# Weighing four value parts of eight on VectorE instead of three, in a two-layer decode kernel

## The chip, the cores and the metric

The kernel runs on one core of one Trainium2 chip. The metric is the time of one execution in device microseconds. The kernel before takes 2680.91 us (median of 3 runs, 2680.71 to 2681.0).

## What is computed

Two layers run one behind the other, each an attention block over a cache and a gated MLP, for two sequences with one new token each; both layers use the same weights and the same cache.

```python
def _A_ref(x, k_cache, v_cache, wq, wo):          # B=2, H=32, Sk=8192, Dh=128, D=576
    q = (x @ wq).reshape(B, Sq, H, Dh).transpose(0, 2, 1, 3)
    scores = einsum("bhqd,bhkd->bhqk", q, k_cache) * (Dh ** -0.5)
    p = softmax(scores, axis=-1)
    o = einsum("bhqk,bhkd->bhqd", p, v_cache)
    return o.transpose(0, 2, 1, 3).reshape(B, Sq, H * Dh) @ wo

def _B_ref(x, w_gate, w_up, w_down):              # Df=4608
    return (gelu(x @ w_gate) * (x @ w_up)) @ w_down

x = x + _A_ref(layernorm(x), ...);  x = x + _B_ref(layernorm(x), ...)
x = x + _A_ref(layernorm(x), ...);  x = x + _B_ref(layernorm(x), ...)
```

All is float32. The two caches hold 2 x 32 x 8192 x 128 numbers each, 268 MB apiece, and each layer reads both from HBM.

## The kernel before

**Items.** The attention of a layer is cut into 34 items: 30 of two heads of one sequence (item numbers 0 to 29) and 4 of one head. The first layer takes them in rising order, the second in falling order, and a few singles at the turn stay on the chip. For an item of two heads, each of the 128 partitions holds 128 rows of the keys (half of the partitions for each head), 128 x 128 numbers, in 8 parts of 16 rows. Keys and values of an item come with one transfer each, on SyncE's queue (`load`, L168), into one large tile, `space`. It has three places for such a block, each a pair of slots, and a transfer is issued when its whole pair is free. The keys of item i+1 go where the values of item i-2 were, the values of item i where its own keys were. The program is written out in order for each engine, and no scheduler changes that order.

**Keys.** `multiply` (L738) takes an item's keys in three units of 3, 3 and 2 parts. VectorE multiplies a unit with the query, which stands spread over all partitions in PSUM (L769), GpSimd adds the upper half of each row to the lower (L798), and VectorE sums what is left of each row (`add_up`, L801). The sum of one unit is taken after the product of the next one. The last unit's sum comes at the head of the next item's work, together with the maximum (`peak`, L825). The exponentials (`softmax`, ScalarE, L858) give the weights `prz`.

**Values, five parts of eight.** TensorE multiplies the weights with the values (`values`, L943): one product for each 4 of a partition's 128 rows, so 4 for a part, and 20 for five parts. In the profile each product of this kind is two rows.

**Values, the other three parts.** For the items that `folds` names (L893: items 3 to 26 in the first layer, 2 to 26 in the second, 49 together) VectorE weighs the rows of the last three parts with their weights (`weigh`, L911), which ScalarE has copied into the PSUM tile `share` (L905, in `bank2`), and GpSimd folds them: it halves the number of rows again and again (L914) until 4 are left, and adds the two results (L916). TensorE then adds up these 4 rows over the partitions with one product (`folded`, L921), which also sets the parts' place free. `weigh` is called twice for an item: with `first` behind the next item's third key product, and without it one item later, behind the last sum of the keys.

**Around it.** Item i's block in the loop (L1051) first sums the last unit of the keys of item i-1 and weighs for item i-2 (second call). Then it takes the three key units of item i, with the query of the next item and the folded product of item i-2 behind the first unit, the values of item i-1 and in every second item the gathering of a finished pair (L966, L967) behind the second, and the first call of `weigh` for item i-1 behind the third.

Of the kernel before, what the change touches and what calls it, by code (L numbers as in the profile page):

```python
# [24 lines left out]
JC = 16  # L25
# [18 lines left out]
END = RING + NPLACE * PLACE  # L44
HELD = 5
SPLIT = (18, 18, 12, 16)
FOLD = 3


class Item:  # L50
# [75 lines left out]
def decode_layers(ctx, tc, x_in, kc, vc, wq, wo, wg, wu, wd, out):  # L126
# [32 lines left out]
    def part_at(at, n):  # L159
        return space[:, at:at + n]  # L160
# [177 lines left out]
    def groups(layer):  # L338
        return range(H // WIDE[layer])[::1 - 2 * layer]

    def name(kind, layer, n):

        return kind, 1 if n in (KEYS_HELD if kind == "k" else VALUES_HELD) else layer, n
# [119 lines left out]
    for b in range(B):  # L463
        rows = ident.rearrange("p (c v i r) -> p i r v c", c=4, v=4, i=2)[:, :, :, b, :]
# [51 lines left out]
    low = bank2[:, 4 * GH + P + 6:]  # L516
    share = low[:, :FOLD * JC]
    kept = psum1.tile([P, JC, DH], F32, name="kept")
# [93 lines left out]
    def attention(layer):  # L612
# [224 lines left out]
        def weights_of(n):  # L837

            if ITEMS[n].heads == 2:
                return prz.rearrange("p a e -> p (a e)")  # L840
            return prz[:, n - PAIRS, :]
# [55 lines left out]
        def weigh(n, first):  # L897

            lo = ITEMS[n].parts - FOLD
            if first:  # L900
                of_halves = weights_of(n)[:, 8 + 4 * JC * lo:8 + 4 * JC * (lo + FOLD)]
                of_halves = of_halves.rearrange("p (g a e) -> p a g e", a=4, e=4)
                for i in range(2):
                    at = slice(i * HALF, i * HALF + HALF)
                    nc.scalar.copy(share[at].rearrange("p (g e) -> p g e", e=4), of_halves[at, i])  # L905
            begin, rows = (0, JC) if first else (JC, (FOLD - 1) * JC)
            at = arena.live[name("v", layer, n), lo][0]
            t = part_at(at, FOLD * PART).rearrange("p (j d) -> p j d", d=DH)
            of_rows = share[:, begin:begin + rows].unsqueeze(2).to_broadcast([P, rows, DH])
            u = t[:, begin:begin + rows]  # L910
            nc.vector.tensor_tensor(out=u, in0=u, in1=of_rows, op=ALU.mult)  # L911
            while rows > 4:
                rows //= 2
                nc.gpsimd.tensor_tensor(out=u[:, :rows], in0=u[:, :rows], in1=u[:, rows:2 * rows], op=ALU.add)  # L914
            if not first:
                nc.gpsimd.tensor_tensor(out=t[:, :4], in0=t[:, :4], in1=u[:, :4], op=ALU.add)  # L916

        def folded(n):

            key, lo = name("v", layer, n), ITEMS[n].parts - FOLD  # L920
            nc.tensor.matmul(  # L921
# [129 lines left out]
        for i, n in enumerate(seq):  # L1051
# [8 lines left out]
            first = layer == 1 and i == 1  # L1060
# [8 lines left out]
            if f is not None:  # L1069
                weigh(f, False)  # L1070
# [3 lines left out]
            for j, (k, m) in enumerate(us):  # L1074
# [28 lines left out]
                if j == 2 and i and folds(p):  # L1103
                    weigh(p, True)
# [14 lines left out]
        first, second = groups(layer)[:2]  # L1119
# [183 lines left out]
```

## Time and profile before

| | |
|---|---|
| median of 3 runs | 2680.91 us |
| the profiled execution | 2680.4 us, its span 2678.6 us |
| TensorE products, weight loads | busy 32%, 10% of the span |
| VectorE | 78% |
| GpSimd | 67% |
| ScalarE | 7% |
| DMA | 1153.33 MB at 431 GB/s on average, busy in tenths 9 or more in 39 of 40 slices |

In the tables by stage, each row gives the stretch in us from the start of the span, its length, the busy time of PE, PEld, DVE (VectorE), ACT (ScalarE) and POOL (GpSimd) with the number of instructions, TensorE's granted clock, the share of the DMA engines that was busy and GB/s. In a timeline, each row has the start, the duration, the engine, the line, the operation, output and inputs, the shape, and in brackets how long the engine was idle before and what ended that. SPq is SyncE's queue of transfers.

### The profile page before, as it was taken

How to read it: one execution, taken by the hardware profiler on the slowest of the kernel's cores; microseconds unless marked ns; L12 is line 12 of the kernel's file. 1: busy time of each engine (PE TensorE's matmuls, PEld its weight loads, DVE VectorE, ACT ScalarE, POOL GpSimd, SP SyncE). 2: the span in 40 equal slices, each digit the busy share in tenths (PEclk: the TensorE clock that was granted, in tenths of full speed). 3: DMA queues.
4: the chain of work that ended last, by engine and by line, in shares of the span. 5: the costliest groups of instructions: out<-in, count | busy, mean ns of one | idle time of the engine just before them, and what ended most of it. 6: DMA issues, size and time to landing. Idle time of an engine off the chain costs nothing.

```text
span 2678.6 us, 14389 instructions
## 1 busy us (share of the span) xinstructions
PE 848.9 (32%) x5550; PEld 269.3 (10%) x5550; DVE 2086.9 (78%) x916; ACT 185.0 (7%) x890; POOL 1797.4 (67%) x559
## 2 busy tenths in 40 slices
PE   1313232232223232334663322223222322222256
PEld 0100000000000000011221100000000000000022
DVE  4878888898888888867038779888888988888840
ACT  0000000000000000001026000000000000000000
POOL 2547787778778777844028458778887877787720
PEclk8666655665665566566986665566566556655678
DMA  9999999999999999999999999999999999999998
GB/s 423 437 429 434 435 433 433 433 436 433 431 435 434 430 436 431 434 429 426 419 417 432 435 437 429 434 434 433 433 433 436 430 433 437 428 436 436 430 431 383
DMA packets 29340, 1153.33 MB, mean 431 GB/s; under 512 B 3384, under 2 KB 3416, under 8 KB 4184
## 3 DMA queue, kind: packets, MB, share of 16 engines
q1 hardware_dynamic: 29088, 1152.40, 99.8%
q8 instruction: 43, 0.70, 0.1%
q14 instruction: 25, 0.20, 0.0%
q10 hardware_dynamic: 184, 0.02, 0.0%
HBM read 1152.39 MB, written 0.01 MB: 430 GB/s over the span
## 4 chain that ended last, share of the span: by engine, by line
DMA 70%; DVE 20%; PE 6%; POOL 3%; issue 1%; ACT 1%; SPq 0%; another core or an unknown queue 0%; POOLq 0%; ACTq 0%; DVEq 0%
DMA space<-in_A_k_cache_dram 61%; DVE space L769 17%; PE acc L921 3%; DMA space<-in_B_w_down_dram 2%; DMA space<-in_B_w_gate_dram 2%; DVE scores L801 2%; POOL space L798 2%; PE bank L687 2%; DMA space<-in_A_v_cache_dram 1%; DMA space<-in_B_w_up_dram 1%; PE bank L1262 1%; DMA space<-in_A_wo_dram 1%; ACT space L791 0%; DMA x<-in_A_x_dram 0%; POOL space L785 0%
## 5 line engine op out<-in xcount | busy, mean ns | idle before, releaser
L798 POOL TENSOR_TENSOR space<-space 128x3072 f32<-128x3072 f32 (+4 forms) x221 | 1128.7, 5108 | 371.2 <-DVE space L769 323.9
L769 DVE TENSOR_TENSOR space<-space,bank 128x6144 f32<-128x6144 f32 (+4 forms) x223 | 1111.9, 4987 | 320.9 <-DMA space<-in_A_k_cache_dram 245.8
L914 POOL TENSOR_TENSOR space<-space 128x1024 f32<-128x1024 f32 (+2 forms) x245 | 575.3, 2348 | 241.2 <-DVE space L911 229.7
L943 PE MATMUL acc<-space,prz 128*16 128x512 f32 (+1 forms) x2920 | 472.7, 812 | 430.2 <-DMA space<-in_A_v_cache_dram 422.1
L801 DVE TENSOR_REDUCE scores<-space 128x48 f32<-128x3072 f32 (+4 forms) x223 | 564.1, 2548 | 23.1 <-POOL space L798 22.9
L911 DVE TENSOR_TENSOR space<-space,bank 128x2048 f32<-128x2048 f32 x98 | 328.3, 3350 | 24.7 <-PE bank L827 24.7
L943 PEld LDWEIGHTS acc<-space,prz 128*16 128x16 f32 (+1 forms) x2920 | 98.1, 120 | 746.5 <-issue 496.8
L687 PE MATMUL bank<-qsb,home 36*128 36x128 f32 x60 | 23.4, 491 | 415.8 <-DVE space L769 397.8
L687 PE MATMUL bank<-qsb,wide 36*128 36x128 f32 x60 | 23.1, 486 | 400.3 <-DVE space L769 383.1
L850 ACT ACTIVATE nbs<-bank 128x2 f32<-128x2 f32 (+1 forms) x68 | 11.6, 171 | 1917.2 <-PE bank L835 1867.5
L585 POOL TENSOR_TENSOR rstd<-ve,few 128x1 f32<-128x1 f32 x4 | 2.2, 561 | 169.0 <-DVE ve L583 169.0
L827 PE MATMUL bank<-ident,m 128*1 128x128 f32 x68 | 21.8, 320 | 273.2 <-DVE m L825 273.1
L921 PE MATMUL acc<-space,few 128*16 128x512 f32 x98 | 92.5, 1047 | 14.2 <-POOL space L916 14.2
L1214 DVE STREAM_TRANSPOSE gu<-acc 128x288 f32<-128x288 f32 x4 | 1.9, 483 | 94.4 <-ACT acc L1212 94.4
L916 POOL TENSOR_TENSOR space<-space 128x512 f32<-128x512 f32 x49 | 62.1, 1267 | 3.8
L687 PEld LDWEIGHTS bank<-qsb,home 36*128 36x128 f32 x60 | 14.7, 304 | 424.8 <-DVE space L769 405.7
L687 PEld LDWEIGHTS bank<-qsb,wide 36*128 36x128 f32 x60 | 14.5, 300 | 408.8 <-DVE space L769 390.3
L858 ACT ACTIVATE prz<-scores,nbs 64x128 f32<-64x128 f32 (+1 forms) x128 | 50.7, 396 | 12.3 <-POOL prz L848 8.9
L791 ACT ACTIVATE space<-space 128x128 f32<-128x128 f32 x164 | 48.4, 296 | 19.7 <-DVE space L769 16.6
L589 DVE TENSOR_TENSOR x<-bank,x 128x144 f32<-128x144 f32 x4 | 1.2, 308 | 57.8 <-PE bank L1262 40.2
L980 PE MATMUL bank<-few,home 128*64 128x4 f32 (+2 forms) x136 | 17.1, 249 | 86.9 <-DVE home L967 86.9
L966 DVE TENSOR_TENSOR acc<-acc,few 128x512 f32<-128x512 f32 x34 | 23.5, 691 | 26.5 <-PE acc L943 26.5
(117 smaller groups left out, 602.8 us busy)
## 6 DMA issues: line engine op xcount, KB each, us to landing
space<-in_A_v_cache_dram SPq DMA_DIRECT2D x7, 4096.0 KB
space<-in_A_k_cache_dram SPq DMA_DIRECT2D x6, 4096.0 KB
space<-in_B_w_gate_dram SPq DMA_DIRECT2D x9, 1152.0 KB
space<-in_B_w_up_dram SPq DMA_DIRECT2D x9, 1152.0 KB
space<-in_B_w_down_dram SPq DMA_DIRECT2D x8, 1152.0 KB
space<-in_A_wq_dram SPq DMA_DIRECT2D x9, 1024.0 KB
space<-in_A_wo_dram SPq DMA_DIRECT2D x2, 4608.0 KB
space<-in_A_k_cache_dram SPq DMA_DIRECT2D x4, 2048.0 KB
```

Source lines behind the costliest of these rows:

```text
L687: nc.tensor.matmul(qb[n], of_row, qsb[rows, m * DH:(m + 1) * DH], start=True, stop=True)
L769: nc.vector.tensor_tensor(out=u[:, :r, :], in0=t[:, :r, :], in1=qb[n].unsqueeze(1).to_broadcast([P, r, DH]), op=ALU.mult)
L791: nc.scalar.activation(u[:, j, :], u[:, j, :], AF.Copy, accum_out=S[n][:, base(n, k) + j:base(n, k) + j + 1])
L798: nc.gpsimd.tensor_tensor(out=half, in0=half, in1=u[:, :r, DH // 2:], op=ALU.add)
L801: nc.vector.tensor_reduce(out=S[n][:, base(n, k):base(n, k) + own_rows(n, k, m)], in_=prod.pop((n, k)), axis=AX.X, op=ALU.add)
L858: nc.scalar.activation(pr[at, lo:].rearrange("p (g e) -> p g e", e=4)[:, 0:it.rows // 2 * it.heads:2 * it.heads, :], s[at, :it.rows].rearr ...
L911: nc.vector.tensor_tensor(out=u, in0=u, in1=of_rows, op=ALU.mult)
L914: nc.gpsimd.tensor_tensor(out=u[:, :rows], in0=u[:, :rows], in1=u[:, rows:2 * rows], op=ALU.add)
L916: nc.gpsimd.tensor_tensor(out=t[:, :4], in0=t[:, :4], in1=u[:, :4], op=ALU.add)
L921: nc.tensor.matmul(accumulator(n)[0:16, :], owner[:, 8 * ITEMS[n].b:8 * ITEMS[n].b + 16], part_at(arena.live[key, lo][0], 4 * DH), start=F ...
L943: nc.tensor.matmul(accumulator(n)[32 * c:32 * c + m, :], pr[:, at:at + m], t[g // 4][:, g % 4 * 4:g % 4 * 4 + 4, :].rearrange("p j d -> p ...
L1262: nc.tensor.matmul(xps[32 * c:32 * c + (2 * B if split else 17), :], hidden(v, e, i), w[:, k, c * CW:(c + 1) * CW], start=(n == 0 and k == ...
```

## The change

The constant FOLD goes from 3 to 4, and both calls of `weigh` take half of the rows. The first call took 16 rows of a partition (one part) and the second 32; both now take 32. The halving loop in `weigh` does the rest. `values` leaves 4 x FOLD of 32 products out, so 16 remain instead of 20, and `share` has 64 columns instead of 48. Lines behind L905 have a number that is higher by one after the change (L911 is L912 there, L914 is L915, L916 is L917, L921 is L922, L943 is L944).

```diff
@@ -44,7 +44,7 @@
 SPLIT = (18, 18, 12, 16)
-FOLD = 3
+FOLD = 4
@@ -903,7 +903,8 @@
                     nc.scalar.copy(share[at].rearrange("p (g e) -> p g e", e=4), of_halves[at, i])
-            begin, rows = (0, JC) if first else (JC, (FOLD - 1) * JC)
+            rows = FOLD // 2 * JC
+            begin = 0 if first else rows
             at = arena.live[name("v", layer, n), lo][0]
             t = part_at(at, FOLD * PART).rearrange("p (j d) -> p j d", d=DH)
             of_rows = share[:, begin:begin + rows].unsqueeze(2).to_broadcast([P, rows, DH])
```

On VectorE, from an item's third key product to the next item's second, before:

```order
L769 TENSOR_TENSOR space<-space,bank 128x4096
L911 TENSOR_TENSOR space<-space,bank_125 128x2048
L801 TENSOR_REDUCE scores<-space 128x48
L801 TENSOR_REDUCE scores<-space 128x32
L825 TENSOR_REDUCE m<-scores 128x1
L911 TENSOR_TENSOR space<-space,bank_125 128x4096
L769 TENSOR_TENSOR space<-space,bank 128x6144
```

And after the change:

```order
L769 TENSOR_TENSOR space<-space,bank 128x4096
L912 TENSOR_TENSOR space<-space,bank_125 128x4096
L801 TENSOR_REDUCE scores<-space 128x48
L801 TENSOR_REDUCE scores<-space 128x32
L825 TENSOR_REDUCE m<-scores 128x1
L912 TENSOR_TENSOR space<-space,bank_125 128x4096
L769 TENSOR_TENSOR space<-space,bank 128x6144
```

Nothing has moved; the first weighing takes twice the elements, ahead of the two last sums.

On GpSimd, from the third add of halves to the next item's first two, before:

```order
L798 TENSOR_TENSOR space<-space 128x32x64
L914 TENSOR_TENSOR space<-space 128x1024
L914 TENSOR_TENSOR space<-space 128x512
L914 TENSOR_TENSOR space<-space 128x2048
L914 TENSOR_TENSOR space<-space 128x1024
L914 TENSOR_TENSOR space<-space 128x512
L916 TENSOR_TENSOR space<-space 128x512
L798 TENSOR_TENSOR space<-space 128x48x64 x2
```

And after the change:

```order
L798 TENSOR_TENSOR space<-space 128x32x64
L915 TENSOR_TENSOR space<-space 128x2048
L915 TENSOR_TENSOR space<-space 128x1024
L915 TENSOR_TENSOR space<-space 128x512
L915 TENSOR_TENSOR space<-space 128x2048
L915 TENSOR_TENSOR space<-space 128x1024
L915 TENSOR_TENSOR space<-space 128x512
L917 TENSOR_TENSOR space<-space 128x512
L798 TENSOR_TENSOR space<-space 128x48x64 x2
```

The first fold has one more add, of 2048 elements, at its head; the rest is as it was.

## The prediction

> **What bounds the kernel now.** I read the busy shares and the 40 slices of the page first, then the chain of waits, then a table by stage over the two long stretches, then the timeline of one item on each engine.
>
> ```profile
> PE 848.9 (32%) x5550; PEld 269.3 (10%) x5550; DVE 2086.9 (78%) x916; ACT 185.0 (7%) x890; POOL 1797.4 (67%) x559
> ...
> DMA  9999999999999999999999999999999999999998
> ...
> DMA 70%; DVE 20%; PE 6%; POOL 3%; issue 1%; ACT 1%; SPq 0%; another core or an unknown queue 0%; POOLq 0%; ACTq 0%; DVEq 0%
> ...
> 219.74:1111.65 891.91, 244.88 (x1151) 71.09 (x1151) 781.29 (x267) 48.06 (x209) 709.39 (x208) 0.59 1.00 433
> 1608.73:2500.61 891.88, 246.17 (x1151) 71.19 (x1151) 781.28 (x267) 48.05 (x209) 709.14 (x208) 0.59 1.00 433
> ```
>
> The first row gives VectorE 78% and GpSimd 67%, the second has the transfers at 9 tenths or more almost throughout, and by the third 70% of the chain of waits is transfers. The last two rows are the stretches in which items of two heads are folded, 23 items each; their columns are the busy times of PE, its weight loads, VectorE, ScalarE and GpSimd, then the clock, the share of the DMA engines and GB/s. The DMA share is 1.00 in both, at 433 GB/s. So the transfers set the time. Each stretch lasts 891.9 us, that is 891.9 / 23 = 38.78 us an item, while VectorE works 781.3 / 23 = 33.97 us of it and GpSimd 30.8 us. Nothing that only frees an engine can shorten this; the change can matter only if it makes a transfer start late. One item shows how much room there is:
>
> ```profile
> 645.92 6.55 DVE L769 TENSOR_TENSOR space<-space,bank 128x6144 f32<-128x6144 f32 x1 [2.81 <-DMA space<-in_A_k_cache_dram]
> ...
> 653.36 6.55 DVE L769 TENSOR_TENSOR space<-space,bank 128x6144 f32<-128x6144 f32 x1 [0.70 <-PE bank L687]
> ...
> 659.92 3.32 DVE L801 TENSOR_REDUCE scores<-space 128x48 f32<-128x3072 f32 x1
> 663.16 4.41 DVE L769 TENSOR_TENSOR space<-space,bank 128x4096 f32<-128x4096 f32 x1
> 667.49 2.28 DVE L911 TENSOR_TENSOR space<-space,bank 128x2048 f32<-128x2048 f32 x1
> 669.69 5.54 DVE L801 TENSOR_REDUCE scores<-space 128x48 f32<-128x3072 f32 x2
> ...
> 676.00 4.42 DVE L911 TENSOR_TENSOR space<-space,bank 128x4096 f32<-128x4096 f32 x1 [0.45 <-PE bank L827]
> 684.62 6.55 DVE L769 TENSOR_TENSOR space<-space,bank 128x6144 f32<-128x6144 f32 x1 [4.20 <-DMA space<-in_A_k_cache_dram]
> ...
> 699.87 3.34 DVE L801 TENSOR_REDUCE scores<-space 128x48 f32<-128x3072 f32 x1
> ```
>
> This is VectorE over one item: keys land at 645.92 and at 684.62 (38.70 us later; 38.78 is the mean with the odd slow transfer). VectorE idles 2.81 us before the one and 4.20 us before the other, since every second item also gathers the products of a finished pair, which puts its first sum 15.25 us after the landing (684.62 to 699.87) and not 14.00. The queue's own rows follow:
>
> ```profile
> 637.94 0.33 SPq L168 DMA_DIRECT2D space<-in_A_v_cache_dram  x1
> 655.17 0.33 SPq L168 DMA_DIRECT2D space<-in_A_k_cache_dram  x1
> 675.25 0.33 SPq L168 DMA_DIRECT2D space<-in_A_v_cache_dram  x1
> ...
> 653.25 1.89 PE L921 MATMUL acc<-space,few 128*16 128x512 f32 x2
> ...
> 665.29 6.71 PE L943 MATMUL acc<-space,prz 128*16 128x512 f32 x40 [7.69 <-DMA space<-in_A_v_cache_dram]
> ```
>
> Values are asked for when the keys' last sum has freed their place: at 637.94, while the keys ahead in the queue land at 645.92, so 7.98 us early; in the other kind of item at 675.25, 9.37 us early. Keys are asked for when the folded product L921 is done: 655.17, while the values ahead land at 665.29, 10.12 us early. The smallest reserve is thus 7.98 us.
>
> **The change, part by part.** On VectorE the weighing behind the third key product grows from 2048 to 4096 elements; the other one keeps its size. The rows give 2.28 and 4.42 us, so +2.14 us an item, ahead of the last sums. On GpSimd the fold that follows it grows from adds of 1024 and 512 to adds of 2048, 1024 and 512:
>
> ```profile
> 643.19 8.29 POOL L914 TENSOR_TENSOR space<-space 128x2048 f32<-128x2048 f32 x3 [4.64 <-DVE space L911]
> 651.56 1.26 POOL L916 TENSOR_TENSOR space<-space 128x512 f32<-128x512 f32 x1
> 652.79 6.70 POOL L798 TENSOR_TENSOR space<-space 128x3072 f32<-128x3072 f32 x1
> 659.99 6.70 POOL L798 TENSOR_TENSOR space<-space 128x3072 f32<-128x3072 f32 x1 [0.50 <-DVE space L769]
> 667.65 4.57 POOL L798 TENSOR_TENSOR space<-space 128x2048 f32<-128x2048 f32 x1 [0.96 <-DVE space L769]
> 672.18 3.69 POOL L914 TENSOR_TENSOR space<-space 128x1024 f32<-128x1024 f32 x2
> 680.50 8.28 POOL L914 TENSOR_TENSOR space<-space 128x2048 f32<-128x2048 f32 x3 [4.63 <-DVE space L911]
> 688.86 1.27 POOL L916 TENSOR_TENSOR space<-space 128x512 f32<-128x512 f32 x1
> ```
>
> That is 8.3 instead of 3.7 us, +4.6 us an item. TensorE loses four of twenty value products (eight of its forty rows); it waits for values before them (7.69 us in the row above), so that is worth nothing, and it frees no place earlier, because keys go into a pair of slots whose second half is released by L921, before and after. ScalarE's two copies of the weights get 64 columns instead of 48:
>
> ```profile
> 660.09 0.43 ACT L905 COPY bank<-prz 64x48 f32<-64x48 f32 x2 [3.13 <-DVE rinv L877]
> ```
>
> They are done at 660.52, 7 us ahead of the weighing that reads them, so a few hundredths more are hidden.
>
> The longer fold itself is covered: it runs from 672.2 to 680.5, and the second fold cannot start before 680.50 + 2.14. What counts is the **loop through both engines**, which I follow from the first sum of an item to the first sum of the next one. From that sum (659.92) to the second weighing (676.00) it is 16.08 us, now 18.22. From there to the second fold 4.50 (676.00 to 680.50), to the last add 8.36 (680.50 to 688.86), to the next add of halves, where GpSimd comes straight from the one to the other, 1.23 (651.56 to 652.79), that add 6.70. The sum behind it starts 0.04 us after GpSimd is done, as here (1133.38 + 4.56 = 1137.94):
>
> ```profile
> 1133.38 4.56 POOL L798 TENSOR_TENSOR space<-space 128x2048 f32<-128x2048 f32 x1 [0.97 <-DVE space L769]
> 1137.98 2.29 DVE L801 TENSOR_REDUCE scores<-space 128x32 f32<-128x2048 f32 x1 [1.41 <-POOL space L798]
> ```
>
> The loop takes 18.22 + 4.50 + 8.36 + 1.23 + 6.70 + 0.04 = **39.05 us**; before it took 36.91, and the key landings at 38.70 set the pace. So after the change the first sum comes 39.05 - 38.78 = 0.27 us later against the transfers in every item. That is hidden while the reserve of the value transfer lasts. The reserve is 7.98 - 2.14 = 5.84 us in the first folded item that gathers, less the time from asking to data. No transfer in the middle of the program starts on an empty queue, so I bound that time by the kernel's first one, asked for at 0.74:
>
> ```profile
> 0.74 0.39 SPq L257 DMA_DIRECT2D space<-in_A_wq_dram  x1
> ...
> 1.24:1.74 0.50, 0.00 (x0) 0.00 (x0) 0.34 (x3) 0.00 (x0) 0.06 (x1) 1.00 0.00 0
> 1.74:2.24 0.50, 0.00 (x0) 0.00 (x0) 0.47 (x5) 0.00 (x0) 0.00 (x0) 1.00 2.98 901
> ...
> 2.74:3.24 0.50, 0.00 (x0) 0.00 (x0) 0.43 (x4) 0.00 (x0) 0.00 (x0) 1.00 0.20 82
> ```
>
> Nothing before 1.74, the last engines between 2.74 and 3.24: 1.0 to 2.5 us. I take 1.75, the middle, since the last of the 16 engines counts but most start early. The reserve is then 4.09 us. The first layer has 24 weighings, 22 of them behind the first that gathers: 22 x 0.27 = 5.94, less 4.09, is 1.85 us of dry queue. The second layer has 25: 6.21 - 4.09 = 2.12. Together **4.0 us**, paid in full because the rest of the program is bound by transfers too. The reserve of the keys stays out of it: L921 waits for the fold, some 2 us later than now plus the drift, of 10.12.
>
> The Trainium skill (DMA: Bandwidth & Descriptors, Latency and other measured facts) puts the first byte of a transfer issued from SP at about 600 ns. By an estimate from that page the reserve would be 5.24 us and the loss 0.70 + 0.97 = 1.7 us; the start of this program shows 1.0 us at the least, so the rows speak for more.
>
> The profiled execution took 2680.4 us, 1.8 of it outside its span of 2678.6; with 4.0 more it is 2684.4. The median of the runs is 0.5 higher, 2680.9, so I forecast **2684.9 us**.
>
> **The rivals.** *The queue never runs dry*: 2680.9 to 2681.5. It needs a loop 0.09 us shorter (22 x 0.18 = 4.0), for instance if a step that I took from rows in which engines waited is shorter when they run back to back. For it speaks that the needed reserve and the reserve at hand differ by 2 us in 6; against it, that adds and weighings repeat to 0.01 us in these rows. A rule of the Trainium skill would have it so (Perfetto Trace Analysis, Identifying the Most-Contended Engine): rank by occupancy or memory use and work on the first. Here that is the transfers, untouched by the change, and the result would be this case's; that VectorE's idle time ends with the keys (2.81 and 4.20 us) agrees for before, but a loop of 39.05 us needs neither engine to be full.
>
> *The loop is longer than summed* (the other side: slower): VectorE and GpSimd now overlap where they did not, the second weighing with the tail of the first fold, and a stretch of that would go into every item. It decides from 39.08 us: each 0.1 us more costs 22 + 23 tenths, 4.5 us. At 39.15 the time is 2689.4, at 39.2 it is 2691.7. For it: the second weighing (676.00 to 680.42) has GpSimd idle beside it in the rows above. Against it: that weighing of 4096 elements takes 4.42 us, and the key product of as many (663.16), with GpSimd's add of 6.70 us from 659.99 on beside it, 4.41.
>
> *The end of the second layer* (slower too): with the reserve used up, the first sum of the last folded item comes 15.25 + 4.09 = 19.3 us after its keys instead of 14.0, and its first weighing takes 2.14 longer, so the last fold comes 7.5 us later than now.
>
> ```profile
> 2529.94 17.26 SPq L168 DMA_DIRECT2D space<-in_A_v_cache_dram  x2
> ...
> 2539.32 2.29 DVE L769 TENSOR_TENSOR space<-space,bank 128x2048 f32<-128x2048 f32 x1 [4.11 <-DMA space<-in_A_k_cache_dram]
> ```
>
> The second of these issues ends at 2547.20, held by the last L921. Keys land at 2539.32, and the values ahead need half of 38.7 us, to 2558.7. At 2554.7 it would still be 4.0 us early, over the 1.75 needed. If drift and start are 5 us worse together, it costs some 3 us on top: 2688.
>
> *Faster* would need transfers of more than 433 GB/s: no mechanism in the profile.
>
> **How the numbers follow.** The loop decides late, 2682 to 2686: 0.46. Never dry: 0.22. Loop longer: 0.25. End of the layer: 0.05. Faster: 0.02. A measurement of this kernel can tell about 0.2%, 5.4 us, from no change. The forecast of +4.0 lies inside it, so same is 0.46 + 0.22 = 0.68, slower 0.30, faster 0.02. The range runs from never dry, 2680.5, to a loop 0.1 longer with a start of 2.5 us (2689.4 + 2 x 0.75 = 2690.9, and a little of the end): 2691.5.
>
> **What would show it right or wrong.** Right: in the first items of each folded stretch VectorE's idle time before the keys shrinks to nothing; then VectorE waits for GpSimd ahead of the first sum (L801 from L798), first sums follow each other at 39.05 us, and late in the stretch the DMA share falls just under 1.00. Wrong: VectorE still waits for keys in the last folded items (loop shorter than the transfers), adds or weighings with other durations than here, or a dry queue in the middle of a stretch.

## The result, and the profile after

| | before | after |
|---|---|---|
| median | 2680.75 us (2680.36 to 2681.0, 6 runs) | 2696.44 us (2695.78 to 2697.83, 6 runs) |
| profiled execution, its span | 2680.4 us, 2678.6 us | 2696.39 us, 2694.6 us |

After to before: **1.0059**, 95% interval 1.0046 to 1.0072. The change costs 15.7 us, where 4.0 were forecast. The whole interval lies above 1, and 2696.44 us lies above the upper end of the forecast's range, 2691.5.

The page of the profile after, its chain of waits and some of its groups, and the two stretches in which items are folded (columns as in the prediction):

```profile
PE 814.0 (30%) x5158; PEld 258.9 (10%) x5158; DVE 2195.7 (81%) x916; ACT 186.3 (7%) x890; POOL 2016.2 (75%) x608
...
DVE 46%; POOL 30%; DMA 18%; issue 3%; PE 2%; ACT 1%; POOLq 0%; SPq 0%; ACTq 0%; DVEq 0%
...
L801 DVE TENSOR_REDUCE scores<-space 128x48 f32<-128x3072 f32 (+4 forms) x223 | 565.2, 2553 | 100.2 <-POOL space L798 100.2
...
L827 PE MATMUL bank<-ident,m 128*1 128x128 f32 x68 | 24.5, 361 | 531.1 <-DVE m L825 531.0
...
L922 PE MATMUL acc<-space,few 128*16 128x512 f32 x98 | 92.5, 1046 | 125.1 <-POOL space L917 125.1
```

```profile
220.38:1120.34 899.96, 226.98 (x967) 65.86 (x967) 832.29 (x267) 48.65 (x209) 811.61 (x230) 0.56 1.00 429
1616.77:2516.53 899.76, 225.83 (x967) 65.67 (x967) 832.30 (x268) 48.66 (x209) 811.21 (x230) 0.57 1.00 429
```

The chain tells most: before, 70% of it was transfers; now 76% is VectorE and GpSimd by turns, and transfers are 18%. Neither engine is full: in the first stretch VectorE works 832.29 of 899.96 us (92%), GpSimd 811.61 (90%). The two rows of stretches are 8.05 and 7.88 us longer than before, which is all of the 15.7 us (15.9). Their DMA share still reads 1.00; only the rate shows it, 429 GB/s after 433. VectorE's wait for GpSimd ahead of the first sums is 100.2 us in all. The same groups of before:

```profile
L801 DVE TENSOR_REDUCE scores<-space 128x48 f32<-128x3072 f32 (+4 forms) x223 | 564.1, 2548 | 23.1 <-POOL space L798 22.9
...
L827 PE MATMUL bank<-ident,m 128*1 128x128 f32 x68 | 21.8, 320 | 273.2 <-DVE m L825 273.1
L921 PE MATMUL acc<-space,few 128*16 128x512 f32 x98 | 92.5, 1047 | 14.2 <-POOL space L916 14.2
```

The timeline after, first where the folded stretch begins, then deep in it:

```profile
220.38 6.55 DVE L769 TENSOR_TENSOR space<-space,bank 128x6144 f32<-128x6144 f32 x1 [1.97 <-DMA space<-in_A_k_cache_dram]
...
259.07 6.55 DVE L769 TENSOR_TENSOR space<-space,bank 128x6144 f32<-128x6144 f32 x1 [0.69 <-DMA space<-in_A_k_cache_dram]
...
940.94 3.35 DVE L801 TENSOR_REDUCE scores<-space 128x48 f32<-128x3072 f32 x1 [1.18 <-POOL space L798]
...
948.53 4.41 DVE L912 TENSOR_TENSOR space<-space,bank 128x4096 f32<-128x4096 f32 x1
...
958.43 0.33 SPq L168 DMA_DIRECT2D space<-in_A_v_cache_dram  x1
958.44 0.29 DVE L825 TENSOR_REDUCE m<-scores 128x1 f32<-128x128 f32 x1
...
958.87 0.37 PE L827 MATMUL bank<-ident,m 128*1 128x128 f32 x1 [10.47 <-DVE m L825]
959.28 4.42 DVE L912 TENSOR_TENSOR space<-space,bank 128x4096 f32<-128x4096 f32 x1 [0.56 <-PE bank L827]
963.67 6.55 DVE L769 TENSOR_TENSOR space<-space,bank 128x6144 f32<-128x6144 f32 x1
963.78 8.31 POOL L915 TENSOR_TENSOR space<-space 128x2048 f32<-128x2048 f32 x3 [2.31 <-DVE space L912]
...
972.17 1.27 POOL L917 TENSOR_TENSOR space<-space 128x512 f32<-128x512 f32 x1
973.39 13.35 POOL L798 TENSOR_TENSOR space<-space 128x3072 f32<-128x3072 f32 x2
...
980.11 3.35 DVE L801 TENSOR_REDUCE scores<-space 128x48 f32<-128x3072 f32 x1 [2.06 <-POOL space L798]
```

VectorE's idle time before the keys is 1.97 us in the first item that gathers, then 0.69, and by 336.64, the fourth item of the stretch, it is gone: from there to the end of the stretch VectorE never waits for keys (963.67 has no wait). The first sums stand 980.11 - 940.94 = **39.17 us** apart. Step by step: 18.34 from the first sum to the second weighing, 4.50 to the second fold, 8.39 to its last add, 1.22 to the next add of halves, 6.72 to the next first sum. This is the forecast loop, 0.12 us longer than summed, and 0.10 to 0.11 of that is one place: the transpose L827 of the maxima lasts 0.37 us, and VectorE waits 0.56 us for it where the prediction's row had 0.45. The traces tell what goes with the longer transpose. These are the stretches of three transposes; the last three columns are the granted clock, the DMA share and GB/s. Two are from before, the first of them in the item that the prediction summed:

```profile
675.69:675.96 0.27, 0.27 (x1) 0.05 (x1) 0.00 (x0) 0.00 (x0) 0.18 (x1) 1.00 0.56 243
598.29:598.66 0.37, 0.37 (x1) 0.05 (x1) 0.00 (x0) 0.00 (x0) 0.17 (x1) 0.50 0.41 177
```

One is from after:

```profile
958.87:959.24 0.37, 0.37 (x1) 0.05 (x1) 0.00 (x0) 0.00 (x0) 0.37 (x1) 0.50 0.41 177
```

The transpose lasts 0.27 us where TensorE's granted clock is 1.00, and 0.37 where it is 0.50. That holds for all 136 of both traces but three, which stand within 0.1 us of a change of the clock. In the two folded stretches of before, half of the transposes met the full clock (23 of 46), with TensorE idle for 3.0 to 5.7 us ahead of them; after, none of 46 did, and the idle time ahead was 7.7 to 11.1 us (531.1 instead of 273.2 us in all, in the groups above).

### The profile page after: what moved, and what is told of

The parts are those of the page before. It is cut to its first block, busy times and chain, and to the rows that moved or that the text cites. A ratio compares the mean times of both kernels' runs of the same rounds, so it can differ in the third digit from the quotient of the medians.

```text
span 2694.6 us, 13655 instructions
## 1 busy us (share of the span) xinstructions
PE 814.0 (30%) x5158; PEld 258.9 (10%) x5158; DVE 2195.7 (81%) x916; ACT 186.3 (7%) x890; POOL 2016.2 (75%) x608
## 4 chain that ended last, share of the span: by engine, by line
DVE 46%; POOL 30%; DMA 18%; issue 3%; PE 2%; ACT 1%; POOLq 0%; SPq 0%; ACTq 0%; DVEq 0%
DVE scores L801 16%; DVE space L912 15%; POOL space L915 14%; DVE space L769 13%; POOL space L798 13%; DMA space<-in_A_k_cache_dram 11%; DMA space<-in_B_w_down_dram 3%; POOL space L917 2%; DMA space<-in_B_w_gate_dram 2%; DMA space<-in_A_wo_dram 1%; DMA space<-in_B_w_up_dram 1%; PE bank L827 1%; DVE m L825 1%; ACT space L791 0%; PE acc L1187 0%
## 5 line engine op out<-in xcount | busy, mean ns | idle before, releaser
L915 POOL TENSOR_TENSOR space<-space 128x2048 f32<-128x2048 f32 (+2 forms) x294 | 797.8, 2714 | 128.2 <-DVE space L912 112.8
L801 DVE TENSOR_REDUCE scores<-space 128x48 f32<-128x3072 f32 (+4 forms) x223 | 565.2, 2553 | 100.2 <-POOL space L798 100.2
L944 PE MATMUL acc<-space,prz 128*16 128x512 f32 (+1 forms) x2528 | 428.1, 842 | 317.6 <-DMA space<-in_A_v_cache_dram 309.4
L912 DVE TENSOR_TENSOR space<-space,bank 128x4096 f32<-128x4096 f32 x98 | 433.0, 4418 | 27.2 <-PE bank L827 27.2
L827 PE MATMUL bank<-ident,m 128*1 128x128 f32 x68 | 24.5, 361 | 531.1 <-DVE m L825 531.0
L944 PEld LDWEIGHTS acc<-space,prz 128*16 128x16 f32 (+1 forms) x2528 | 86.8, 123 | 599.3 <-issue 426.2
L922 PE MATMUL acc<-space,few 128*16 128x512 f32 x98 | 92.5, 1046 | 125.1 <-POOL space L917 125.1
L917 POOL TENSOR_TENSOR space<-space 128x512 f32<-128x512 f32 x49 | 62.1, 1268 | 3.8
L827 PEld LDWEIGHTS bank<-ident,m 128*1 128x1 f32 x68 | 5.4, 79 | 588.2 <-issue 533.8
L687 PEld LDWEIGHTS bank<-qsb,wide 36*128 36x128 f32 x60 | 14.5, 299 | 325.3 <-DVE space L769 310.5
```

The lines of the kernel that those rows point to most:

```text
L687: nc.tensor.matmul(qb[n], of_row, qsb[rows, m * DH:(m + 1) * DH], start=True, stop=True)
L801: nc.vector.tensor_reduce(out=S[n][:, base(n, k):base(n, k) + own_rows(n, k, m)], in_=prod.pop((n, k)), axis=AX.X, op=ALU.add)
L827: nc.tensor.transpose(mT[n], m, ident)
L922: nc.tensor.matmul(accumulator(n)[0:16, :], owner[:, 8 * ITEMS[n].b:8 * ITEMS[n].b + 16], part_at(arena.live[key, lo][0], 4 * DH), start=F ...
L944: nc.tensor.matmul(accumulator(n)[32 * c:32 * c + m, :], pr[:, at:at + m], t[g // 4][:, g % 4 * 4:g % 4 * 4 + 4, :].rearrange("p j d -> p ...
```

## Experiments

Three theories were set against each other. **A**: the loop through VectorE and GpSimd is longer than the transfers of an item, and the loss begins when the reserve of the value request is used up. **B**: the value request simply comes later, behind a longer weighing. **C**: the added work on GpSimd as a whole costs, wherever it lies.

### The loop alone: more GpSimd work in the kernel before

Three kernels add only useless adds to the second fold of the kernel *before* (three parts, short first weighing), at the place where the loop passes. The largest, with adds of 1024 and 512 elements:

```diff
             if not first:
+                nc.gpsimd.tensor_tensor(
+                    out=u[:, 16:16 + 8], in0=u[:, 16:16 + 8], in1=u[:, 24:24 + 8], op=ALU.add
+                )
+            if not first:
+                nc.gpsimd.tensor_tensor(
+                    out=u[:, 16:16 + 4], in0=u[:, 16:16 + 4], in1=u[:, 24:24 + 4], op=ALU.add
+                )
+            if not first:
                 nc.gpsimd.tensor_tensor(out=t[:, :4], in0=t[:, :4], in1=u[:, :4], op=ALU.add)
```

The other two have the add of 1024 alone, and one of 512 alone. The added adds write rows that nothing reads.

> The kernel before with two more GpSimd adds, of 1024 and 512 elements, on rows that nobody reads any more, between the second fold and its last add: 3.65 us. Theory A: the loop is 40.7 us, 1.92 over the transfers, 45 x 1.92 - 6.6 = 80 us: 2761 us. Rival C: less than the change's loss, since less GpSimd work is added than the 4.6 us of the change: up to 2693 us.

> The kernel before (three parts) with one more GpSimd add of 1024 elements, on rows that nobody reads any more, between the second fold and its last add: 2.35 us. VectorE's work and its request for values are those of before. Theory A: the loop of before, 36.91 us by the rows of before and 37.04 with the 0.13 us that the change's trace adds, becomes 39.4 us, 0.66 over the transfers' 38.78, and a reserve of 7.98 less some 4.7 us is used up per layer: 45 x 0.66 - 2 x 3.3 = 23 us, 2704 us. Rival B: the weighing ahead of the request is the old one, 2681 us. Rival C: half of the change's added GpSimd work, so at most half of the change's loss, 2681 to 2689 us.

Measured: **2757.21 us** for 1024 + 512 (2756.46 to 2758.5; ratio 1.0286, interval 1.027 to 1.0301) and **2695.26 us** for 1024 (2693.26 to 2695.42; ratio 1.0052, 1.0035 to 1.0069). The larger one, in its timeline:

```profile
1035.26 2.36 POOL L916 TENSOR_TENSOR space<-space 128x1024 f32<-128x1024 f32 x1
1037.70 1.27 POOL L920 TENSOR_TENSOR space<-space 128x512 f32<-128x512 f32 x1
1038.93 1.27 POOL L924 TENSOR_TENSOR space<-space 128x512 f32<-128x512 f32 x1
1040.15 13.37 POOL L798 TENSOR_TENSOR space<-space 128x3072 f32<-128x3072 f32 x2
...
1046.86 3.35 DVE L801 TENSOR_REDUCE scores<-space 128x48 f32<-128x3072 f32 x1 [3.25 <-POOL space L798]
...
1067.40 6.55 DVE L769 TENSOR_TENSOR space<-space,bank 128x6144 f32<-128x6144 f32 x1
```

The two adds of 2.36 and 1.27 us lie in the path to the first sum, VectorE waits 3.25 us for GpSimd there, and the next keys (1067.40) are not waited for. In the trace the items follow each other at 40.56 us. That is 1.78 over the 38.78 of the transfers; over 45 items it is 80 us, and 76.4 were paid. So 3.65 us of GpSimd work that touches neither weighing nor request costs 76 us: C's price is far too low, B has no place in it, and A stands. The expectation for the smaller one, 2704, was too high: the loop came out at 39.23 us, not 39.4 as summed. C's bound of 2689 is missed there too.

> The kernel before with one more GpSimd add of 512 elements on rows that nobody reads any more, between the second fold and its last add: 1.27 us. Theory A: the loop is 38.3 to 38.4 us, under the transfers' 38.78 on average: no loss, 2681 us, 2682 at most. Rival C: 1.27 of the change's 4.6 us of added GpSimd work, 2685 us.

With 512 alone the time is 2684.6 us (2682.81 to 2686.12, 10 runs; ratio 1.0013, 1.0004 to 1.0023). That misses A's 2681 to 2682 and is C's number, 2685. But in its trace the keys of the folded stretches keep their pace except beside two items, which is not how a cost in every item would look; those two are taken up below.

### The first fold is covered

The kernel after, without the first add (2048 elements) of the first fold, which is the only one that the change added. The result lacks those rows.

```diff
             nc.vector.tensor_tensor(out=u, in0=u, in1=of_rows, op=ALU.mult)
+            if first:
+                rows //= 2
             while rows > 4:
```

> The change with the new add of 2048 elements left out of the first fold, so that half of the rows of the first weighing are missing in the result. GpSimd's work is that of the kernel before, VectorE's that of the change. Theory A: the first fold lies beside the last sums and the second weighing and is not in the loop; the loop stays 39.18 us and the time 2696 us, within 1 us. Rival B: 2696 us too. Rival C: GpSimd has its old load, 2681 to 2684 us.

Measured: 2696.92 us (2696.16 to 2697.98; ratio 1.0061, 1.0046 to 1.0076). The 4.6 us of added GpSimd work per item are worth nothing, as the prediction had it: the second fold waits for the second weighing anyway. C falls here a second time.

### The request alone: how early must values be asked for?

In the kernel before, the second weighing is put ahead of the last sum. The work is the same, the loop is not longer, but the request for the values goes out some 4.3 us later.

```diff
+            if f is not None:
+                weigh(f, False)
             if first or ahead:
                 add_up(p, *units(p)[-1])
                 peak(p)
-            if f is not None:
-                weigh(f, False)
```

> The kernel before with the second weighing (4.42 us) moved ahead of the last sum of the keys, so that values are asked for 4.34 us later; the work of all engines is the same and the loop is not longer. This measures the time from asking to data by itself: 7.98 - 4.34 = 3.64 us are left ahead of the keys' landing in every second item, 5.03 in the others. With the 1.75 us of the prediction the queue never runs dry: 2681 us. With some 4.7 us, as the change's own loss would need, each of about 24 items that gather loses 1.06 us: 2706 us. Rival B, which takes late asking for the whole cause, expects at least twice the change's loss, since the request is twice as late: 2712 us or more.

Measured: **2700.05 us** (2698.72 to 2701.92; ratio 1.0073, 1.0058 to 1.0088). Requests and next keys in its timeline:

```profile
2080.72 0.33 SPq L168 DMA_DIRECT2D space<-in_A_v_cache_dram  x1
2086.91 6.55 DVE L769 TENSOR_TENSOR space<-space,bank 128x6144 f32<-128x6144 f32 x1 [5.90 <-DMA space<-in_A_k_cache_dram]
...
2121.84 0.33 SPq L168 DMA_DIRECT2D space<-in_A_v_cache_dram  x1
2125.61 6.55 DVE L769 TENSOR_TENSOR space<-space,bank 128x6144 f32<-128x6144 f32 x1 [3.48 <-DMA space<-in_A_k_cache_dram]
...
2159.27 0.33 SPq L168 DMA_DIRECT2D space<-in_A_v_cache_dram  x1
2166.93 6.55 DVE L769 TENSOR_TENSOR space<-space,bank 128x6144 f32<-128x6144 f32 x1 [7.36 <-DMA space<-in_A_k_cache_dram]
```

VectorE waits for keys in every item here, so the loop is not the bound. At 2080.72 the values were asked for 6.19 us ahead of the keys' landing, and the next keys followed 38.70 us later. At 2121.84 it was 3.77 us ahead, and the next keys came after 41.32, so 2.62 us were lost. Over all items between 219 and 2481 us: with a lead of under 4.0 us (20 items, 3.77 on average) the next keys came 0.86 us late on average, from 0.0 to 2.62; with leads of 4.22, 4.49 and 4.72 us they came 0.46, 0.36 and 0.05 late; with a lead of 5.0 to 6.8 us (22 items) 0.11 us late, near the 0.08 us that odd slow transfers cost before. So a request has to go out some 3.77 + 0.86 = **4.6 us** ahead of the landing that VectorE sees, not the 1.75 us of the prediction. This figure is an average: single items scatter widely. By the values of the expectation this is the case of 4.7, which gave 2706; the loss was smaller, 20 items at 0.86 us and not 24 at 1.06.

The packets of the transfers, as the trace records them for the 16 DMA engines, show what the 4.6 us are made of. Each engine carries its own share of a transfer, 8 packets of 64 KB, and a packet of 4 bytes marks its end; the table has the ends of a key transfer, in us:

```
                          values      first engine  last engine  VectorE's keys  the earliest value packets
                          asked for   ends keys     ends keys    start           last
before                    675.25      682.09        684.12       684.62          2.42
after                     958.43      960.18        963.18       963.67          2.78, 2.85, 2.88, 2.70; 2.42 from 961.46 on
weighing ahead of the sum 2121.84     2122.82       2125.15      2125.61         3.15, 3.00, 3.10, 3.13; one 3.92 at 2124.88
```

In the kernel before, the engines end 2.03 us apart, and VectorE starts 0.50 us after the last: the first engine needs values 2.53 us ahead of the landing that VectorE sees. From the request on, it took 2.2 to 3.0 us until packets had their usual 2.42 us again, with the exception of the one at 2124.88. The two together are 4.7 to 5.5 us.

Once in the kernel with the weighing put ahead, the request came when 10 engines had already ended the keys, the first at 2200.95. The queue's row and three stretches around it (the whole of a packet counts in the stretch in which it starts, so a share can be over 1):

```profile
2201.86 0.33 SPq L168 DMA_DIRECT2D space<-in_A_v_cache_dram  x1
```

```profile
2201.00:2202.00 1.00, 0.00 (x0) 0.00 (x0) 0.96 (x2) 0.00 (x0) 1.00 (x1) 0.50 0.01 0
2202.00:2202.50 0.50, 0.21 (x1) 0.08 (x1) 0.15 (x1) 0.00 (x0) 0.50 (x1) 0.50 0.00 0
2202.50:2203.00 0.50, 0.17 (x1) 0.00 (x0) 0.00 (x0) 0.00 (x0) 0.50 (x1) 0.50 3.77 1311
```

The value packets of the 15 engines that stood empty start 2202.81 to 2203.51, 0.95 to 1.65 us after the request, and last 2.6 to 3.4 us. On average they end 1.8 us later than packets of the usual 2.42 us that began at the request itself. So 1.75 us was a good value for the time from asking to data. Counted from the first engine's end, 1.8 + 2.53 gives 4.3 us, and with the 4.7 to 5.5 above it encloses the 4.6.

In the last row of the table the engine with 3.92 lost 1.5 us, then another 0.95 us when a packet of 16 KB of another queue came between (2150.55), and it ended the next keys at 2166.48, when the other 15 had ended by 2163.83: a landing waits for the slowest engine, and what one of them loses is not shared out. An engine counts as busy through the whole of a drawn-out packet, which is why the DMA share stays at 1.00 and the loss shows in the GB/s alone: summed over the 64 KB packets of its first stretch, the kernel after spends 9.8 us per engine above 2.416 us a packet, the kernel before 2.6, and the stretch is 8.05 us longer.

B's own number for this kernel, 2712 or more, is missed too: a request that is 4.3 us later costs 19 us here because it goes below the need in half of the items, while the change's 2.14 us alone leave 5.8, which is enough by the leads above, and by the kernel below that keeps the longer weighing and has a shorter loop. The loop's drift is what takes the rest.

### Values in two transfers, the first half asked for earlier

The values of most folded items come as two transfers of four parts, the first asked for some 2.25 us earlier; in the kernel after, and as a control in the kernel before.

```diff
-            v(n - 1)
+            if 2 < n < PAIRS - 3:
+                by_halves(name("v", 0, n - 1), vc, n - 1, name("k", 0, n - 1))
+            else:
+                v(n - 1)
...
-            cache(("v", 1, n + 1), vc, n + 1)
+            if 0 < n < last - 3:
+                by_halves(("v", 1, n + 1), vc, n + 1, ("k", 1, n + 1))
+            else:
+                cache(("v", 1, n + 1), vc, n + 1)
```

> The change with the values of folded items asked for in two transfers, the first as soon as the first half of the keys' place is free, 2.25 us ahead of the last sum's end. The loop stays 39.18 us. Theory A with a time from asking to data of 4.7 us: the reserve grows from 1.1 to 3.4 us a layer, so 4.5 us less are lost: 2692 us. If the loop alone counted and no reserve, 2696 us; if late asking alone counted, 2681 us.

> The kernel before with values asked for in two transfers in the same way: shows what the cut itself costs. All theories: 2681 us, if transfers of half the size move at the same rate; some us more if each further transfer costs time.

Measured: 2705.87 us (2704.2 to 2708.11; ratio 1.0094, 1.0079 to 1.0109) and 2695.26 us (2694.63 to 2696.9; ratio 1.0056, 1.0039 to 1.0073). Both expectations fail: the control alone lost 14.5 us. Its folded stretch shows where not, and the turn between the layers where:

```profile
219.74:1111.65 891.91, 245.02 (x1151) 68.84 (x1151) 781.25 (x267) 48.06 (x209) 707.88 (x208) 0.58 1.00 433
```

```profile
1150.00:1200.00 50.00, 12.67 (x83) 5.11 (x83) 36.47 (x17) 4.38 (x18) 22.95 (x6) 0.60 0.79 333
```

```profile
1150.00:1200.00 50.00, 19.10 (x123) 6.69 (x127) 40.54 (x19) 4.39 (x18) 27.38 (x7) 0.64 0.98 423
```

The first two rows are the control's, the third is before. In the folded stretch the rate is the same 433 GB/s, but between 1150 and 1200 us the DMA share falls from 0.98 to 0.79, which is 9.5 us of 50. The edit thus also moved something at the turn that it was not meant to move; why, was not looked into. Measured against each other the two cut kernels differ by 10.6 us and the uncut ones by 15.7, so the earlier request gave back 5.1 us (forecast 4.5). By the folded stretches of the profiled executions it is nearer 3: the cut kernels' take 899.94 and 899.81 us against 893.36 and 893.45, 12.9 us together, the uncut ones' 15.9. The direction agrees with a reserve that is used up, the size is not settled by this pair.

### The loop made shorter than the transfers

The kernel after, with the last add of the fold (L917, 1.27 us) taken from GpSimd; TensorE adds up the two folded products instead.

```diff
-            if not first:
-                nc.gpsimd.tensor_tensor(out=t[:, :4], in0=t[:, :4], in1=u[:, :4], op=ALU.add)
...
-            nc.tensor.matmul(
-                accumulator(n)[0:16, :], owner[:, 8 * ITEMS[n].b:8 * ITEMS[n].b + 16],
-                part_at(arena.live[key, lo][0], 4 * DH), start=False, stop=completes(seq.index(n)),
-            )
+            for half in range(2):
+                nc.tensor.matmul(
+                    accumulator(n)[0:16, :], owner[:, 8 * ITEMS[n].b:8 * ITEMS[n].b + 16],
+                    part_at(arena.live[key, lo][0] + half * FOLD // 2 * PART, 4 * DH),
+                    start=False, stop=half == 1 and completes(seq.index(n)),
+                )
```

> The change with GpSimd's last add of the second fold (512 elements, L917) left out: TensorE adds the two results with two folded products in place of one. VectorE's weighings and GpSimd's first fold stay as in the change. Theory A (the loop from one item's first sum through both engines to the next item's first sum, 39.18 us in the change, is longer than an item's transfers, 38.78 us on average): the loop loses 1.22 us, 37.96 us, and is shorter than the transfers again; values are still asked for 5.8 us ahead: 2681 us, as before the change, 2683 at most. Rival B (the longer weighing ahead of the request for values is the cause by itself): the request is as late as in the change, 2696 us. Rival C (GpSimd's added work as a whole): 1.2 of 4.6 us come back, 2692 us.

Measured: 2687.03 us (2683.28 to 2687.92, 10 runs; ratio 1.0022, 1.0012 to 1.0031). Most of the loss is gone, but 6.5 us are left, against A's 2681. The trace has the whole rest at two places, item 15 in the first layer and item 41 (counted through both layers) in the second, with the second key product 13.6 and 14.4 us behind the first instead of 7.44:

```profile
607.40 6.55 DVE L769 TENSOR_TENSOR space<-space,bank 128x6144 f32<-128x6144 f32 x1 [1.56 <-DMA space<-in_A_k_cache_dram]
613.87 0.42 DVE L668 COPY wide<-few 128x128 f32<-128x128 f32 x1
614.17 6.65 POOL L798 TENSOR_TENSOR space<-space 128x3072 f32<-128x3072 f32 x1
614.21 6.69 DVE L668 COPY home<-few 128x128 f32<-128x128 f32 x1
...
621.03 6.53 DVE L769 TENSOR_TENSOR space<-space,bank 128x6144 f32<-128x6144 f32 x1
```

The copy L668, which spreads a sequence's query and runs only where the sequence changes, lasts 6.69 us beside GpSimd's add of 6.65. Before, it fell into a gap of GpSimd and lasted 0.22:

```profile
611.56 1.26 POOL L916 TENSOR_TENSOR space<-space 128x512 f32<-128x512 f32 x1
613.68 0.22 DVE L668 COPY wide<-few 128x128 f32<-128x128 f32 x1
613.82 0.22 DVE L668 COPY home<-few 128x128 f32<-128x128 f32 x1
613.90 6.70 POOL L798 TENSOR_TENSOR space<-space 128x3072 f32<-128x3072 f32 x1 [1.07 <-issue]
```

The Trainium skill (SBUF — State Buffer, Who interferes with whom) says that VectorE, in modes that copies can enter, contends with GpSimd for a shared pair of ports: whichever issues first has it for the whole instruction, and the other is blocked. The trace agrees with that: GpSimd's add starts 0.04 us ahead of the copy, and the copy lasts 6.69 us beside its 6.65. In which mode the copy ran no row shows. The kernel before with the add of 512 shows the same at the same two items. If that copy is all, it can go to ScalarE:

```diff
             for b, to in enumerate(of_batch):
-                nc.vector.tensor_copy(
+                nc.scalar.copy(
```

> The kernel after without the last add of halves (TensorE adds up two products instead), and with the copies of a sequence's query (L668) on ScalarE instead of VectorE. Without the second edit this kernel took 2687.0 us, 6.5 over the kernel before, though its loop through VectorE and GpSimd, about 38.0 us, is shorter than the transfers' 38.78. In its trace every pair of products is 7.4 us apart but two, item 15 of the first layer (13.6 us) and item 41 (14.4 us), where a copy of 128 numbers a partition lasts 6.69 us instead of 0.22 beside an add of GpSimd that lasts 6.65. If that copy, held up by GpSimd, is all of the 6.5 us, the time is that of the kernel before, 2680.8 (2680.3 to 2681.5), and four parts of eight on VectorE cost nothing once the loop is shorter than the transfers. If the two stalls are a symptom only, it stays at 2685 to 2688.

> The kernel before with one more add of 512 elements on GpSimd in the second fold, as tried already (2684.6 us), now with the copies of L668 on ScalarE. Theory of the loop with the copy as the one disturbance: the loop of some 38.15 us is shorter than 38.78, so the time is that of the kernel before, 2680.8 (2680.3 to 2681.5). If 1.27 us more on GpSimd cost something by themselves, 2683 to 2686.

> The kernel after with the copies of L668 on ScalarE. In the kernel after one of the four copies lasts 0.74 us instead of 0.22, so the disturbance that the two other kernels show is hardly there: 2695.5 to 2696.5 if its 15.7 us come from the loop of 39.18 us and the reserve; 2689 or less if the copy, or where it stands, carries a part of them.

Measured, beside 2680.6 us for the kernel before: **2681.55 us** for the first (2681.03 to 2684.19, 11 runs; ratio 1.0004, 0.9996 to 1.0013), 2682.32 us for the second (2681.64 to 2683.86, 11 runs; 1.0007, 0.9998 to 1.0016), 2697.32 us for the third (2696.75 to 2698.77; 1.0063, 1.0049 to 1.0077). The first one where the copy was:

```profile
607.22 6.55 DVE L769 TENSOR_TENSOR space<-space,bank 128x6144 f32<-128x6144 f32 x1 [1.58 <-DMA space<-in_A_k_cache_dram]
...
614.73 6.55 DVE L769 TENSOR_TENSOR space<-space,bank 128x6144 f32<-128x6144 f32 x1 [0.76 <-PE bank L687]
```

The second product is back at 7.51 us behind the first. With four parts of eight weighed on VectorE, a loop of some 38 us and the copy out of the way, the kernel comes within 1 us of the one before. All three medians lie above the expected ranges, by 0.05, 0.8 and 0.8 us; the second lies between its two expectations. The intervals of the first two include 1, but nearly all of their runs are above the 21 of before (2680.41 to 2681.14), so 1.0 and 1.7 us are left. In the profiled executions of these two the keys of the first layer's folded stretch start within 0.9 us of before, most within 0.3, and 1.5 and 3.2 us come in between the layers; why was not looked into. In the kernel after, moving the copy gives back nothing of the 15.7 us. None of these beats the kernel before: with the transfers setting the pace there, the work moved between the engines won nothing.

## Why the prediction was right in kind and wrong in size

- **What bounds the kernel, and where the change bites: right.** Idle time before the keys shrinks and disappears, VectorE waits for GpSimd ahead of L801, and the loss is only in the folded stretches.
- **The first fold is covered: right**, shown by leaving its first add out (2696.92 us).
- **The loop: right as a mechanism, 0.13 us short.** The steps gave 39.05, the items follow each other at 39.17 to 39.18. This was the rival "the loop is longer than summed", but its reason was not the one named there: weighings and adds kept their durations to 0.02 us. It was the transpose L827, whose row of before the sum had taken from one item, one in which the granted clock was 1.00. Over the 68 the times are 0.27 to 0.37 us before, with a median of 0.31, and after the median is 0.37, at a clock of 0.50. Worth 45 x 0.13 = 5.9 us. The change takes value products off TensorE, and its idle time ahead of the transpose grows; that this lowers the clock fits the rows above, but no run holds the one and changes the other. By the prediction's own rate the longer loop makes 2684.9 + 5.9 = 2690.8 us, still 5.6 short.
- **The reserve of the value request: wrong, and it is the other half.** The prediction counted 7.98 - 2.14 = 5.84 us from the request to the landing that VectorE sees, and took off 1.75 us, the time from asking to data at the kernel's first transfer. That time was well chosen (1.8 us on average where the engines stood empty). What the step left out is that the first of the 16 engines has ended the keys 2.53 us before VectorE sees them. The need is then about 4.6 us, and 20 requests under 4.0 us ahead lost 0.86 us each. The step from 1.75 to 4.6 is worth 2 x 2.85 = 5.7 us. The trace of after shows the reserve run out early. 5.84 - 4.6 = 1.2 us last for three items at 0.4 us each, and the 16 engines end the keys of the first four items of the stretch 38.7 to 38.8 us apart (mean of the engines), those of the fifth 38.85 and of the sixth 39.14 us after the ones before; by the prediction, 4.09 us would have lasted for 15 items at 0.27. A dry queue in the middle of a stretch was one of its signs of being wrong. The kernels' times point the same way, more loosely: with a loop of 39.18 the kernel after pays 45 x 0.40 = 18.0 us less twice its reserve; 15.7 paid means 1.15 us of reserve a layer, a need of 5.84 - 1.15 = 4.7. In the same way the kernel before with the add of 1024 gives 5.2, and with 1024 + 512 6.1.
- **Both together**: 4.0 + 5.9 + 5.7 = 15.6 us, against 15.7 measured. That it fits to 0.1 us is partly luck: with needs of 4.6 to 5.2 us the sum is 15.6 to 16.8. The Trainium skill's figure of about 600 ns for a first byte (DMA: Bandwidth & Descriptors, Latency and other measured facts) put the loss at 1.7 us, further off. The earliest value packets on engines that stood empty start 0.95 us after the request (2201.86 to 2202.81).
- **Never dry: wrong.** Its condition, a loop 0.09 us shorter, is the wrong way round. The Trainium skill's rule beside it (Perfetto Trace Analysis, Identifying the Most-Contended Engine) would, as the prediction read it, work on the transfers first, but the chain of after is 76% VectorE and GpSimd, though they are busy 92% and 90% of the stretch.
- **The end of the second layer: right** that it costs nothing; the two stretches carry 15.9 of 15.7 us.
- **The sign that the DMA share would fall just under 1.00: wrong.** It stays at 1.00 with 429 instead of 433 GB/s.

The range was too narrow for the same reason: its upper end took the loop 0.1 us longer, where 0.13 came, but never a need above 2.5 us, since the time between the first engine's end and the landing was not in the sum.

## What to carry to other kernels

Work added to two engines that hand data back and forth is priced by the loop through both, against the period of whatever sets the pace: below it the cost here was about nothing (1.0 us with the copy out of the way), above it the excess is paid in every round, 0.4 us times 45 here. In this kernel the reserve ahead of the transfer queue ran out when the first DMA engine was out of work, not when the consumer saw the landing: 2.5 us earlier, to be taken off along with the time from asking to data. A row read from one item can hide a spread: look at all of its kind before it goes into a sum that is paid 45 times. And a single short instruction that used to fall into a gap of another engine is worth a look whenever the gap closes.

## What was not expected of the hardware

- A VectorE copy of 128 numbers a partition between two places in SBUF took 6.69 us instead of 0.22 beside a GpSimd add, twice in a whole execution; without it that kernel was 5.5 us faster (2687.03 and 2681.55).
- The 16 DMA engines end one 8 MB transfer 2.0 us apart in the undisturbed kernel (682.09 to 684.12), and an engine that has lost 0.9 us to a packet of another queue stays behind the others for the transfers that follow: in after the last engine ends at 963.18 and the last but one at 961.83, and on the next transfer of keys or values at 982.54 and 981.15.
- The first packets behind a late request are drawn out, to as much as 3.9 us instead of 2.42 in the requests of the table, most of them on engines that went straight on from the keys.
- The transpose L827 of 128 numbers takes 0.27 us at a granted clock of 1.00 and 0.37 at 0.50, in before with both in one execution and with the longer one in all folded items after.
